# Hash attention and feed-forward on one core: another start of attention, and hash bits on column halves kept on the chip in place of column quarters placed by transfers

## The chip, the cores and the metric

The kernel runs on one core of one Trainium2 chip. The metric is the device time of one execution in microseconds (us); the time before is the median of three runs. The engines are TensorE (PE, matrix products; PEld is its weight load), VectorE (DVE), ScalarE (ACT), GpSimd (POOL) and SyncE (SP, which here only issues transfers). Each engine works through its own instructions in order and waits on semaphores for the others.

## The reference, cut to what matters

```python
batch, n_heads, seq, head_dim = (4, 8, 768, 64)      # q, k, v; proj is 64 x 6
q_bits = (np.einsum('bhsd,dk->bhsk', q, proj) > 0)   # 6 hash bits of each query
k_bits = (np.einsum('bhsd,dk->bhsk', k, proj) > 0)   # and of each key
q_bucket = np.sum(q_bits * 2 ** np.arange(6), axis=-1)
k_bucket = np.sum(k_bits * 2 ** np.arange(6), axis=-1)
mask = q_bucket[:, :, :, None] == k_bucket[:, :, None, :]
scores = np.where(mask, scale * np.matmul(q, k.transpose(0, 1, 3, 2)), -1e9)
attn = softmax(scores)                               # over the keys
x = np.matmul(attn, v)                               # then reshaped to 3072 x 512
# feed-forward: n_tokens, d_model, d_ff = (3072, 512, 2048)
h = x @ w_in
g = h * erf(softplus(h))
out = g @ w_out
```

## The kernel before

The heads are worked on in 16 pairs (a and b). q and k of a pair lie one head on partitions 0 to 63, the other on 64 to 127. A half is 384 of the 768 queries, HS = 384. A score block is 128 keys by 384 queries of both heads; a pair has 12 of them. Each block is four matrix products in one PSUM tile: two that put the mask there, made of bits, and two in fp32 with q and k. ACT takes the exp of it, and the product with v (`weigh`) sums over the keys. The score tiles and the bits share one ring of three PSUM tiles.

```python
QR = 32
QB = QR // 2
WARM = 7
...
nc.vector.memset(w_sum[:, 0, 0, 0:HS], 1.0)
warm = w_sum[:, 0, 0, 0:HS].bitcast(BF16)
proj_in = const.tile([P, 2 * NBIT], F32, name="proj_in")
nc.scalar.dma_start(out=proj_in, in_=proj2)
...
def fetch(i, load, quick=False):
    ...
    for half in range(2 if quick else 1):
        cols = slice(half * HS, half * HS + HS) if quick else slice(0, S)
        for n, what in enumerate("qk"):
            queue = nc.scalar if quick and what == "k" and half == 0 else nc.sync
            for ab in range(2):
                queue.dma_start(...)
    # then v, by nc.sync
```

The first pair takes its bits on column halves, one half of the sequence after the other: two products into the tile `bits` (q to partitions 0 to 63, k to 64 to 127), the sign by ACT, and three small DVE operations.

```python
def hash_bits(d, big, halves=(0, 1)):
    if halves[0] == 0:
        d["bits"] = big("bits")
    for half in halves:
        for n, what in enumerate("qk"):
            nc.tensor.matmul(out=d["bits"][n * D : n * D + D, half, 0:HS], lhsT=proj_sb,
                             rhs=d[what][:, half * HS : (half + 1) * HS], start=True, stop=True)

def take_bits(d, tile_of, halves=(0, 1)):
    cols = slice(halves[0] * HS, (halves[-1] + 1) * HS)
    sign_bits(d, tile_of, cols)            # ACT
    for ab in (1, 0):
        spread_bits(d, cols, ab)           # DVE, scaled by a weight
    double_bits(d, cols)                   # DVE copy

def score(n, c):
    ...
    st = d["st", n, c] = big("st")
    for part, src in enumerate(("b", "")):     # "b": mask in bf16, "": q and k in fp32
        for ab in range(2):
            rows = slice(ab * D, ab * D + D)
            nc.tensor.matmul(out=st[:, ab, 0:HS], lhsT=d["k" + src][rows, keys],
                             rhs=d["q" + src][rows, cols], start=(part == 0), stop=(part == 1))
...
pairs[0] = fetch(0, load, quick=True)
for n in range(WARM):
    nc.tensor.matmul(out=bank("warm"), lhsT=warm[:, 0:P], rhs=warm[:, P : P + 512], start=True, stop=True)
for half in range(2):
    hash_bits(pairs[0], big, (half,))
    take_bits(pairs[0], lambda what: both[0][:, "qk".index(what[0]), :], (half,))
```

All later pairs take them on column quarters: four products side by side, one sign, one DVE scaling, a store to memory, and two loads that place the bits where the mask product wants them.

```python
def bits_of(i):
    d["bits"] = big("bits")
    for n, what in enumerate("qk"):
        for half in range(2):
            row = (2 * n + half) * QR
            nc.tensor.matmul(out=d["bits"][row : row + QR, 0, 0:HS], lhsT=proj_q,
                             rhs=d[what][:, half * HS : (half + 1) * HS], start=True, stop=True)

def sign_of(i):      # ACT Sign, 128 x 384, into sg
def weigh_bits(i):   # DVE, sg[64:128] times weight_q
def leave_bits(i):   # POOL queue: sg to memory
def place_bits(i):   # POOL queue: two loads into both[i % 2]
def clean():         # POOL clears both[0] once
```

A list scheduler in the kernel fixes the order of all engines ahead of time from costs that are written in it; PE's own order is a fixed chain, which for half h holds the score blocks, in every other half the bits of the next pair, the divisor of the half before, and `weigh`.

```python
order = [("score", 0)]
for h in range(NH):
    order += [("score", n) for n in (2 * h + 1, 2 * h + 2) if n < NS]
    if h == 0:
        order.insert(3, ("bits", 1))
    if h % 2 and (h + 3) // 2 < NPAIR:
        order.append(("bits", (h + 3) // 2))
    if h >= 1:
        order.append(("divisor", h - 1))
    order += [("weigh", 2 * h), ("weigh", 2 * h + 1)]
```

Beside attention DVE and ACT split the float64 weights into fp32 (32 pieces). The feed-forward follows when attention ends.

Of the kernel before, what the change touches and what calls it, by code (L numbers as in the profile page):

```python
# [193 lines left out]
def kernel(  # L194
# [36 lines left out]
    QB = QR // 2  # L231
    WARM = 7
    proj_sb = const.tile([P, 2 * QR], F32, name="proj_sb")
    weight = const.tile([P, 2], F32, name="weight")
    proj_q = const.tile([P, QR], F32, name="proj_q")
    weight_q = const.tile([P, 1], F32, name="weight_q")
# [12 lines left out]
    warm = w_sum[:, 0, 0, 0:HS].bitcast(BF16)  # L249
    proj_in = const.tile([P, 2 * NBIT], F32, name="proj_in")  # L250
    nc.scalar.dma_start(out=proj_in, in_=proj2)
# [9 lines left out]
    steps = const.tile([P, 8], F32, name="steps")  # L261
    for c, (end, factor) in enumerate(
        (
            (NBIT, NBIT + 1.0),
            (NBIT + 1, -float(NBIT)),
            (QR, -1.0),
            (QR + NBIT, NBIT + 1.0),
            (QR + NBIT + 1, -float(NBIT)),
            (QB, -1.0),
            (QB + NBIT, NBIT + 1.0),  # L270
            (QB + NBIT + 1, -float(NBIT)),
        )
    ):
        nc.vector.tensor_scalar(
            out=steps[:, c : c + 1],
            in0=row,
            scalar1=float(end),
            scalar2=factor * BIG,
            op0=ALU.is_lt,
            op1=ALU.mult,  # L280
        )
    nc.vector.reduce_sum(out=weight[:, 0:1], in_=steps[:, 0:2], axis=AX.X)
    nc.vector.reduce_sum(out=weight[:, 1:2], in_=steps[:, 2:5], axis=AX.X)
    nc.vector.memset(proj_q, 0.0)
    for ab in range(2):
        rows = slice(ab * D, ab * D + D)
        nc.vector.tensor_copy(
            out=proj_q[rows, ab * QB : ab * QB + NBIT],
            in_=proj_in[rows, ab * NBIT : (ab + 1) * NBIT],
        )  # L290
    nc.vector.reduce_sum(out=weight_q, in_=steps[:, 5:8], axis=AX.X)
    nc.vector.tensor_tensor(out=weight_q, in0=weight_q, in1=weight[:, 0:1], op=ALU.add)
    nc.vector.tensor_copy(out=weight_q[D + QR : P, :], in_=weight_q[D : D + QR, :])
# [52 lines left out]
    def fetch(i, load, quick=False):  # L346
        d = dict(
            q=load.tile([P, S], F32, name="q", tag="q"),
            k=load.tile([P, S], F32, name="k", tag="k"),
            v=load.tile([P, NC, P], F32, name="v", tag="v"),  # L350
        )
        b, j = divmod(i, JP)
        for half in range(2 if quick else 1):
            cols = slice(half * HS, half * HS + HS) if quick else slice(0, S)
            for n, what in enumerate("qk"):
                queue = nc.scalar if quick and what == "k" and half == 0 else nc.sync
                for ab in range(2):
                    queue.dma_start(
                        out=d[what][ab * D : ab * D + D, cols],
                        in_=qkT[2 * i + ab, n * D : n * D + D, cols],  # L360
                    )
        for ab in range(2):
            nc.sync.dma_start(
                out=d["v"][:, :, ab * D : ab * D + D],
                in_=v[b, 2 * j + ab].rearrange("(c p) d -> p c d", p=P),
            )
        return d

    def hash_bits(d, big, halves=(0, 1)):
        if halves[0] == 0:  # L370
            d["bits"] = big("bits")
# [10 lines left out]
    def sign_bits(d, tile_of, cols):  # L382

        if cols.start == 0:
            for what in ("qb", "kb"):
                d[what] = tile_of(what)
# [23 lines left out]
    def take_bits(d, tile_of, halves=(0, 1)):  # L410
        cols = slice(halves[0] * HS, (halves[-1] + 1) * HS)
        sign_bits(d, tile_of, cols)
# [4 lines left out]
    def attention():  # L417
        NS = NPAIR * 4
        with (
            tc.tile_pool(name="load", bufs=3) as load,  # L420
            tc.tile_pool(name="bitp", bufs=1) as bitp,
            tc.tile_pool(name="ep", bufs=1) as ep,
            tc.tile_pool(name="xst", bufs=1) as xst,
# [8 lines left out]
            sg = bitp.tile([P, HS], BF16, name="sg")  # L432
            both = [bitp.tile([P, 2, S], BF16, name=f"both{n}") for n in range(2)]
            nc.gpsimd.memset(both[1], 0.0)
# [102 lines left out]
            def score(n, c):  # L537
# [5 lines left out]
                st = d["st", n, c] = big("st")  # L543
                for part, src in enumerate(("b", "")):
                    for ab in range(2):
# [7 lines left out]
                        )  # L553

# [33 lines left out]
            def sum_keys(h, k):  # L588
                i, half = divmod(h, 2)
                d = pairs[i]  # L590
                if k == 0:
                    if h >= NH - 2:
                        if half:
                            room = blocks[1][:, :, :].rearrange("p k t -> p (k t)")[:, 0:S]
                        else:
                            room = load.tile([P, S], F32, name="q", tag="q")
                        d["sum", half] = room.rearrange("p (n a c) -> p n a c", n=1, a=2)
# [34 lines left out]
            def home(i, what):  # L632

                if i < NPAIR - 1:
                    shape, bufs = {"x": (S, 3), "z": (HS, 1), "r": (S, 2)}[what]
                    return xst.tile([P, shape], F32, name=what, tag=what, bufs=bufs)
                rows = blocks[1][:, :, :].rearrange("p k t -> p (k t)")
                c = {"x": S, "z": 2 * S, "r": 0}[what]
                return rows[:, c : c + (HS if what == "z" else S)]
# [132 lines left out]
            for n in range(WARM):  # L772
                nc.tensor.matmul(  # L773
                    out=bank("warm"),
                    lhsT=warm[:, 0:P],
                    rhs=warm[:, P : P + 512],
# [3 lines left out]
            for half in range(2):  # L780
                hash_bits(pairs[0], big, (half,))
                take_bits(pairs[0], lambda what: both[0][:, "qk".index(what[0]), :], (half,))
# [14 lines left out]
            def bits_of(i):  # L797


                d = pairs[i]  # L800
                d["bits"] = big("bits")
                for n, what in enumerate("qk"):
                    for half in range(2):
                        row = (2 * n + half) * QR
                        nc.tensor.matmul(  # L805
                            out=d["bits"][row : row + QR, 0, 0:HS],
                            lhsT=proj_q,
                            rhs=d[what][:, half * HS : (half + 1) * HS],
                            start=True,
                            stop=True,  # L810
                        )

            def sign_of(i):
                nc.scalar.activation(
                    out=sg,
                    in_=pairs[i].pop("bits")[:, 0, 0:HS],
                    func=AF.Sign,
                    scale=2.0**100,
                    bias=sgn[:, 0:1],
                )  # L820

            def weigh_bits(i):

                nc.vector.tensor_scalar(
                    out=sg[D:P, :],
                    in0=sg[D:P, :],
                    scalar1=weight_q[D:P, 0:1],
                    scalar2=None,
                    op0=ALU.mult,
                )  # L830

            def leave_bits(i):
                bd = pairs[i]["bd"] = dram.tile([4, 2, QB, HS], BF16, name="bd", tag="bd")
                nc.gpsimd.dma_start(out=bd.rearrange("n a r c -> (n a r) c"), in_=sg)

            def place_bits(i):

                d = pairs[i]
                bd = d.pop("bd")
                for n, what in enumerate(("qb", "kb")):  # L840
                    d[what] = both[i % 2][:, n, :]
                for ab in range(2):
                    nc.gpsimd.dma_start(
                        out=both[i % 2][ab * D : ab * D + NBIT + 1, :, :].rearrange(
                            "r w (h c) -> r (w h) c", h=2
                        ),
                        in_=bd[:, ab, 0 : NBIT + 1, :].rearrange("n r c -> r n c"),
                    )

            def clean():  # L850

                nc.gpsimd.memset(both[0], 0.0)
# [3 lines left out]
            for h in range(NH):  # L856
                order += [("score", n) for n in (2 * h + 1, 2 * h + 2) if n < NS]
                if h == 0:
                    order.insert(3, ("bits", 1))
                if h % 2 and (h + 3) // 2 < NPAIR:  # L860
                    order.append(("bits", (h + 3) // 2))
# [4 lines left out]
            for what, n in order:  # L866
                if what == "score":
                    i = n // 4
                    after = (("place_bits", i),)
                    for c in range(GC):  # L870
                        free = (slots[-3],) if len(slots) >= 3 else ()
                        pe(score, (n, c), 0.82, after + free)
                        slots.append(("exponential", n, c))
                elif what == "bits":
                    pe(bits_of, (n,), 0.92, (("start_pair", n), slots[-3]))
# [27 lines left out]
            for h in range(NH):  # L903
                for k, (blocks_, _, _, where) in enumerate(sum_steps(h)):
                    after = tuple(("exponential", 2 * h + b // GC, b % GC) for b in blocks_)
                    after += (("sum_keys", h, k - 1), ("sum_keys", h - 1, last_sum(h - 1)))
                    if k == 0:
                        after += (("divisor", h - 2),)
                        if h == NH - 2:
                            after += (("measure", NPAIR - 3, 0, 1),)  # L910
                    op(sum_keys, (h, k), "DVE", 1.72 if where == 2 else 0.92, (1, 2 * h + 1, k), after)
            for h in range(NH - 1):
# [7 lines left out]
                    (("divisor", h), ("spread", i - 1)),  # L920
# [6 lines left out]
            for i in range(NPAIR):  # L927
                n = 4 * i
                if i:
# [10 lines left out]
                    op(sign_of, (i,), "ACT", 0.6, (0, n - 6, 9), (("bits_of", i), ("leave_bits", i - 1)))  # L940
                    op(weigh_bits, (i,), "DVE", 0.33, (0, n - 6, 1), (("sign_of", i),))
                    op(leave_bits, (i,), "POOL", 0.7, (0, n - 6, 2), (("weigh_bits", i),), late=2.6)
                    op(
                        place_bits,
                        (i,),
                        "POOL",
                        1.2,
                        (0, n - 6, 3),
                        (("leave_bits", i), ("score", n - 5, 2)) + (("clean",),) * (i == 2),
                        late=2.6,  # L950
# [11 lines left out]
                if i == NPAIR - 1:  # L962
# [11 lines left out]
                    (("ungather", i), ("normalise", i - 2)),  # L974
# [4 lines left out]
            op(clean, (), "POOL", 1.4, (0, 0), (("score", 3, 2),), late=0.3)  # L979
# [49 lines left out]
    def general():  # L1029

        with (
# [13 lines left out]
            for i in range(NPAIR):  # L1045
# [3 lines left out]
                take_bits(d, lambda what: bitp.tile([P, S], BF16, name=what, tag=what))  # L1049
# [704 lines left out]
```

## Time and profile before

| | |
|---|---|
| time, median of 3 runs | 919.47 us (918.86 to 923.69) |
| span of the profiled run | 917.7 us |
| first score block on PE | 9.58 us |
| first exp on ACT | 11.42 us |
| first product with v on PE | 18.90 us |
| last product with v ends on PE | about 324.6 us |

The page gives the busy time of each engine and its share of the span, the span in slices, and the chain of work that ended last, followed back from the last instruction. A timeline row has start, length, engine, line of the kernel, operation, what is written and read, how many were merged into the row, and in brackets how long the engine sat idle before it and what released it. The row "waits" has who waited for whom, the total in us, the times and the longest. Ends of matrix products are modelled, and merged rows overlap, so starts are safer to compare than lengths.

### The profile page before, as it was taken

The numbers are of one execution on the slowest core, as the hardware profiler recorded it, in microseconds if no ns is written. First come the engines' busy times: TensorE is split into PE (matmuls) and PEld (weight loads), VectorE is DVE, ScalarE is ACT, GpSimd is POOL, SyncE is SP. The second block draws the span as 40 slices with busy tenths as digits, with TensorE's granted clock in tenths as the row PEclk, the third lists the DMA queues.
The fourth block names the chain that finished last, engine by engine and source line by source line (L and its number), as shares of the span: only waits on it lengthen the run. The fifth ranks groups of instructions, "written<-read, shape, count | busy, mean of one in ns | idle before, by whom it ended". The sixth has DMA issues, their size and how long they took to land.

```text
span 917.7 us, 13114 instructions
## 1 busy us (share of the span) xinstructions
PE 904.2 (99%) x5003; PEld 657.1 (72%) x5003; DVE 820.2 (89%) x1020; ACT 768.2 (84%) x1002; POOL 46.1 (5%) x82
## 2 busy tenths in 40 slices
PE   8999999999999999999999999999999999999997
PEld 3444444444444478888888888888888888888885
DVE  4889999999999979899999799989899889988995
ACT  5788887788887839999998998899989997899892
POOL 1211111111111000000000000000000000000000
PEclk9999999999999999999999999999999999999999
DMA  8456567665574231102022112211221021111211
GB/s 205 114 155 163 144 178 194 184 161 164 155 190 138 59 122 64 46 1 104 12 70 80 36 46 69 81 35 46 70 81 35 35 75 40 36 35 46 69 35 49
DMA packets 63078, 83.05 MB, mean 90 GB/s; under 512 B 34286, under 2 KB 47454, under 8 KB 63008
## 3 DMA queue, kind: packets, MB, share of 16 engines
q1 hardware_dynamic: 56672, 64.08, 24.6%
q0 software_dynamic: 6032, 17.86, 6.3%
q8 instruction: 41, 0.67, 0.3%
q10 hardware_dynamic: 304, 0.20, 0.1%
q14 instruction: 29, 0.24, 0.1%
HBM read 64.71 MB, written 17.40 MB: 89 GB/s over the span
## 4 chain that ended last, share of the span: by engine, by line
PE 95%; DVE 2%; ACT 1%; DMA 1%; issue 0%; POOL 0%; DVEq 0%; POOLq 0%
PE M L1313 31%; PE X L1173 28%; PE st L547 16%; PE av L624 14%; PE M L1173 3%; PE z_ps L659 1%; PE bits L805 1%; ACT e_all L561 1%; PE warm L773 0%; DVE e L1227 0%; PE bits L374 0%; DMA bd<-sg 0%; DVE h L1255 0%; DMA both<-bd 0%; DVE S L1270 0%
## 5 line engine op out<-in xcount | busy, mean ns | idle before, releaser
L1240 DVE SCALAR_TENSOR_TENSOR e<-w,e 128x1024 f32<-128x1024 f32 x144 | 173.3, 1219 | 5.8 <-ACT w L1236 3.0
L561 ACT ACTIVATE e_all<-st 128x768 f32<-128x768 f32 x192 | 151.5, 813 | 14.2 <-PE st L547 12.8
L1236 ACT ACTIVATE w<-w,cq 128x1024 f32<-128x1024 f32 x144 | 160.6, 1143 | 1.9
L547 PE MATMUL st<-q,k 64*128 64x384 f32 x768 | 156.1, 485 | 0.0
L1313 PE MATMUL M<-w_out_sb,h 128*128 128x256 f32 x576 | 140.2, 379 | 0.4 <-DVE h L1255 0.4
L624 PE MATMUL av<-e_all,v 128*64 128x385 f32 (+1 forms) x768 | 131.2, 490 | 0.0
L1173 PE MATMUL X<-x,w_in_sb 128*128 128x256 f32 x512 | 121.1, 379 | 0.0
L1313 PEld LDWEIGHTS M<-w_out_sb,h 128*128 128x128 f32 x576 | 109.3, 190 | 15.9 <-DVE h L1255 1.1
L1173 PEld LDWEIGHTS X<-x,w_in_sb 128*128 128x128 f32 x512 | 97.0, 190 | 13.8 <-ACT h L1191 0.6
L624 PEld LDWEIGHTS av<-e_all,v 128*64 128x64 f32 x768 | 52.3, 136 | 67.5 <-issue 65.4
L547 PEld LDWEIGHTS st<-q,k 64*128 64x128 f32 x768 | 68.8, 189 | 35.1 <-issue 34.8
L1313 PE MATMUL M<-wt,S 128*128 128x256 f32 x384 | 93.4, 379 | 0.4 <-DVE S L1270 0.4
L1173 PE MATMUL X<-x_sum,w_sum 128*128 128x256 f32 x344 | 81.7, 380 | 1.8 <-ACT h L1191 1.8
L1313 PEld LDWEIGHTS M<-wt,S 128*128 128x128 f32 x384 | 72.9, 190 | 10.7 <-DVE S L1270 0.8
L1173 PEld LDWEIGHTS X<-x_sum,w_sum 128*128 128x128 f32 x344 | 65.0, 190 | 12.0 <-ACT h L1191 3.3
L1191 ACT COPY h<-X 128x512 f32<-128x512 f32 x85 | 49.1, 577 | 22.3 <-PE X L1173 21.4
L1217 DVE SCALAR_TENSOR_TENSOR w<-w,e 128x1024 f32<-128x1024 f32 x48 | 58.4, 1220 | 9.7 <-ACT w L1212 9.6
L547 PE MATMUL st<-both 64*128 64x384 bf16 x384 | 63.7, 326 | 1.6 <-DMA both<-bd 1.0
L1255 DVE TENSOR_TENSOR h<-h,e 128x1024 f32<-128x1024 f32 x48 | 57.9, 1220 | 5.8 <-ACT e L1251 5.6
L1231 ACT ACTIVATE w<-e 128x1024 f32<-128x1024 f32 x48 | 50.4, 1050 | 13.2 <-DVE e L1227 13.0
L1227 DVE TENSOR_TENSOR e<-e,w 128x1024 f32<-128x1024 f32 x48 | 57.4, 1218 | 2.7 <-ACT e L1223 2.6
L1195 DVE TENSOR_TENSOR h<-X,h 128x512 f32<-128x512 f32 x65 | 44.8, 689 | 16.4 <-PE X L1173 15.4
(132 smaller groups left out, 1373.8 us busy)
## 6 DMA issues: line engine op xcount, KB each, us to landing
wt<-wt SPq DMA_DIRECT2D x24, 768.0 KB, 4.2
raw<-in_w_out_dram POOLq DMA_DIRECT2D x16, 512.0 KB, 4.1
raw<-in_w_in_dram POOLq DMA_DIRECT2D x14, 512.0 KB, 4.9
v<-in_v_dram SPq DMA_DIRECT2D x32, 192.0 KB, 4.7
xs<-x SPq DMA_DIRECT2D x16, 384.0 KB, 3.2
q<-in_qkT_dram SPq DMA_DIRECT2D x30, 192.0 KB, 4.2
k<-in_qkT_dram SPq DMA_DIRECT2D x30, 192.0 KB, 4.5
r<-rd SPq DMA_DIRECT2D x30, 192.0 KB, 3.5
```

What stands on the lines that cost most here:

```text
L547: nc.tensor.matmul(out=st[:, ab, 0:HS], lhsT=d["k" + src][rows, keys], rhs=d["q" + src][rows, cols], start=(part == 0), stop=(part == 1),)
L561: nc.scalar.activation(out=e[:, :, 0:HS], in_=st[:, :, 0:HS], func=AF.Exp, scale=scale)
L624: nc.tensor.matmul(out=d["av"][rows, 0:w], lhsT=d["v"][:, g * GC + c, rows], rhs=e[:, ab, 0:w], start=(g == 0 and c == 0), stop=(g == 1 an ...
L1173: nc.tensor.matmul(out=d[where][:, u, :], lhsT=a[:, kc, f : f + P], rhs=b[:, kc, :], start=(first and u == 0 and kc == 0), stop=(last and ...
L1191: nc.scalar.copy(out=quarter(p, q), in_=st[p][where])
L1217: nc.vector.scalar_tensor_tensor(out=w, in0=w, scalar=-1.0, in1=st[p]["e", v], op0=ALU.add, op1=ALU.subtract)
L1227: nc.vector.tensor_tensor(out=s, in0=s, in1=st[p].pop(("w", v)), op=ALU.subtract)
L1231: nc.scalar.activation(out=z, in_=st[p]["s", v], func=AF.Square)
L1236: nc.scalar.activation(out=q, in_=z, func=AF.Square, bias=cq[:, j : j + 1])
L1240: nc.vector.scalar_tensor_tensor(out=s, in0=st[p].pop(("q", v, j)), scalar=ERF_Q[j][1], in1=s, op0=ALU.add, op1=ALU.mult,)
L1255: nc.vector.tensor_tensor(out=h, in0=h, in1=st[p].pop(("s", v)), op=ALU.mult)
L1313: nc.tensor.matmul(out=banks[name][:, sub, :], lhsT=a[:, u, sub * P : (sub + 1) * P], rhs=b[:, u, :], start=(c == 0 and k == 0), stop=(c = ...
```

## The change: what it does and what it is for

At the start: the warm-up products on constants become fp32 and are five of 256 columns, so that they follow each other with no gaps; the projection is loaded by POOL's queue; the loads of the second half of the first pair take k ahead of q; the first pair's bits go to two PSUM tiles, one for each half, so that the second half's products don't wait for the first half's sign; and the first two score blocks run their fp32 products first and take their masks last, so that PE has work while the bits are made.

For the later pairs it goes back to bits on column halves that stay on the chip: four products of which two run side by side, one sign of 128 x 768, two DVE scalings and one DVE copy. The store, the two loads, the quarter constants and the clears go away. Some buffers become fewer (x from three to two; z and r share two), and the order of a few operations in the scheduler changes with them.

```diff
-    QB = QR // 2
-    WARM = 7
+    WARM = 5
...
-    warm = w_sum[:, 0, 0, 0:HS].bitcast(BF16)
+    warm = w_sum[:, 0, 0, 0:HS]
...
-    nc.scalar.dma_start(out=proj_in, in_=proj2)
+    nc.gpsimd.dma_start(out=proj_in, in_=proj2)
... (steps for the quarters, proj_q and weight_q go away)
-        for half in range(2 if quick else 1):
-            cols = slice(half * HS, half * HS + HS) if quick else slice(0, S)
-            for n, what in enumerate("qk"):
+        parts = ((0, "q"), (0, "k"), (1, "k"), (1, "q")) if quick else ((None, "q"), (None, "k"))
+        for half, what in parts:
...
     def hash_bits(d, big, halves=(0, 1)):
-        if halves[0] == 0:
-            d["bits"] = big("bits")
+        d["bits"] = big("bits")
...
-            tc.tile_pool(name="bitp", bufs=1) as bitp,
+            tc.tile_pool(name="bitp", bufs=2) as bitp,
             tc.tile_pool(name="ep", bufs=1) as ep,
-            tc.tile_pool(name="xst", bufs=1) as xst,
+            tc.tile_pool(name="sums", bufs=2) as sums,
+            tc.tile_pool(name="xst", bufs=2) as xst,
...
-            def score(n, c):
+            def score(n, c, parts=((0, "b"), (1, ""))):
...
-                st = d["st", n, c] = big("st")
-                for part, src in enumerate(("b", "")):
+                if ("st", n, c) in d:
+                    parts = ((1, "b"),)
+                else:
+                    d["st", n, c] = big("st")
+                st = d["st", n, c]
+                for part, src in parts:
...
+            def plain(n, c):
+                score(n, c, ((0, ""),))
...
-                    shape, bufs = {"x": (S, 3), "z": (HS, 1), "r": (S, 2)}[what]
-                    return xst.tile([P, shape], F32, name=what, tag=what, bufs=bufs)
+                    return xst.tile([P, S], F32, name=what, tag="x" if what == "x" else "z")
...
-                    out=bank("warm"),
+                    out=bank("warm")[:, 0 : 2 * P],
                     lhsT=warm[:, 0:P],
-                    rhs=warm[:, P : P + 512],
+                    rhs=warm[:, P:HS],
...
             def bits_of(i):
-                ... four products with proj_q, each to 32 partitions
+                hash_bits(pairs[i], big)
             def sign_of(i):
-                ... Sign of 128 x 384 into sg
-            def weigh_bits(i): ...
-            def leave_bits(i): ...
-            def place_bits(i): ...
-            def clean(): ...
+                sign_bits(pairs[i], bitp, slice(0, S))
+            def weigh_bits(i, ab):
+                spread_bits(pairs[i], slice(0, S), ab)
+            def copy_bits(i):
+                double_bits(pairs[i], slice(0, S))
...
-                if h == 0:
-                    order.insert(3, ("bits", 1))
-                if h % 2 and (h + 3) // 2 < NPAIR:
-                    order.append(("bits", (h + 3) // 2))
+                if h % 2 == 0 and h // 2 + 1 < NPAIR:
+                    order.append(("bits", h // 2 + 1))
...
+                    if n == 0:
+                        for c in range(2):
+                            pe(plain, (n, c), 0.66)
...
-                    (("divisor", h), ("spread", i - 1)),
+                    (("divisor", h), ("send", i - 1) if i == NPAIR - 1 else ("widen", i - 1)),
```

## The prediction

> **What bounds the kernel now.** I read the page's busy row and chain of waits first, then the windows of 20 us over the attention part, the waits of TensorE (PE), the timeline of one pair of heads, and last the timeline of the first 20 us.
>
> ```profile
> PE 904.2 (99%) x5003; PEld 657.1 (72%) x5003; DVE 820.2 (89%) x1020; ACT 768.2 (84%) x1002; POOL 46.1 (5%) x82
> ...
> PE 95%; DVE 2%; ACT 1%; DMA 1%; issue 0%; POOL 0%; DVEq 0%; POOLq 0%
> ```
>
> PE is busy 99% of the span and is 95% of the chain that ended last. Work added to PE's in-order chain is therefore paid in full, and work on another engine is free until PE waits for it. By stretch (columns: stretch, length, busy of PE, PEld, DVE, ACT, POOL with counts, clock, DMA share, GB/s):
>
> ```profile
> 20.00:40.00 20.00, 19.02 (x142) 9.07 (x140) 16.77 (x23) 16.74 (x33) 5.88 (x9) 1.00 0.51 133
> 40.00:60.00 20.00, 20.00 (x148) 9.31 (x150) 18.38 (x28) 17.06 (x32) 3.40 (x6) 1.00 0.52 126
> ...
> 300.00:320.00 20.00, 20.00 (x146) 9.18 (x141) 18.99 (x28) 16.62 (x30) 0.56 (x1) 1.00 0.23 67
> ```
>
> From 40 us to the end of attention (325 us) PE has almost no gap; the only large one is 1 us between 20 and 40 us. Attention alternates halves with a hash product and halves without. The product with v (av) starts each half's last part, so the distance of its starts is a half's length. PE timeline (columns: start, length, instruction):
>
> ```profile
> 275.02 4.10 PE L624 MATMUL av<-e_all,v 128*64 128x385 f32 x24
> ...
> 284.01 0.52 PE L805 MATMUL bits<-q,proj_q 128*32 128x384 f32 x2
> 284.02 0.52 PE L805 MATMUL bits<-k,proj_q 128*32 128x384 f32 x2
> 284.35 0.49 PE L805 MATMUL bits<-q,proj_q 128*32 128x384 f32 x2
> 284.37 0.49 PE L805 MATMUL bits<-k,proj_q 128*32 128x384 f32 x2
> 284.68 0.51 PE L659 MATMUL z_ps<-x_sum,ones 128*32 128x192 f32 x8
> 285.11 4.09 PE L624 MATMUL av<-e_all,v 128*64 128x384 f32 x24
> ...
> 294.55 4.10 PE L624 MATMUL av<-e_all,v 128*64 128x385 f32 x24
> ```
>
> With the hash product a half lasts 285.11 - 275.02 = 10.09 us, without it 294.55 - 285.11 = 9.44 us. The product costs **0.65 us** of PE net. Its four matrix products (q and k, two halves of columns) are two instructions each, and all four run side by side: two rounds of 0.33 us.
>
> The start (PE timeline again):
>
> ```profile
> 1.40 4.45 PE L773 MATMUL warm<-w_sum 128*128 128x512 bf16 x7 [1.40 <-DVE w_sum L248]
> 5.78 0.90 PE L374 MATMUL bits<-q,proj_sb 128*64 128x384 f32 x1
> ...
> 8.03 0.90 PE L374 MATMUL bits<-q,proj_sb 128*64 128x384 f32 x1 [0.71 <-ACT both L387]
> ...
> 9.58 0.50 PE L547 MATMUL st<-both 64*128 64x384 bf16 x2
> 9.88 1.49 PE L547 MATMUL st<-q,k 64*128 64x384 f32 x4
> 11.16 0.53 PE L547 MATMUL st<-both 64*128 64x384 bf16 x2
> 11.48 1.05 PE L547 MATMUL st<-q,k 64*128 64x384 f32 x4
> 12.37 0.32 PE L547 MATMUL st<-both 64*128 64x384 bf16 x2
> ```
>
> Three things are to be seen. The warm-up leaves holes (0.64 us from one to the next for 512 columns). The second half's bits wait for the Sign of the first half, since both halves share one PSUM tile. And PE runs at half pace until about 11.4 us: the same four fp32 products last 1.49 us at 9.88 and 0.81 us from 12.54 on, so the first two score blocks take 2.8 us instead of 1.6.
>
> **What the Trainium skill says.** "TensorE: Matmul & The Clock Gate", Part 3 (packing small matmuls), says that products in different column groups run at the same time. The trace agrees: 10 to 20 ns lie between the starts of q and k quarters. Part 1 of that page says that the array runs at 1.2 GHz until a free-running window of about 3.4 us was busy, then at 2.4. The trace agrees in size: a bits round is 0.69 us at 5.78 us (to 6.47) and 0.33 us at 284. That a warm-up with holes doesn't count as busy fits (7 of them over 4.45 us left PE slow), but this trace alone doesn't prove it. "DMA: Bandwidth & Descriptors", Anatomy of one DMA, puts some 2 us of fixed cost on any transfer; here the bits' trip to memory takes 3.4 us (median) and the trip back 4.0.
>
> **The change, part by part.**
>
> (a) Later pairs (15 of them): hash bits on column halves again. q takes columns 0-63 and k 64-127, so two products run together and not four: two rounds for each half of the sequence, four rounds in all, 4 x 0.33 = 1.3 us instead of 0.65. Added on PE: 0.65 x 15 = **+9.7 us**, all on the path. ACT's Sign grows from 128x384 (0.59 us) to 128x768 (estimate 0.85, from the exp of that shape at 0.81): +0.27 x 15 = 4 us, where ACT has some 3.5 of 20 us free. DVE loses one 64x384 scaling (0.32) and gets two of 64x768 and a copy of 64x768: between 1.2 us (the costs that the kernel's own scheduler is given) and 1.8 us (twice the 0.32 and 0.25 of the short ones); about +0.9 to 1.5 a pair, 13 to 22 us in all. DVE's idle time from 20 to 320 us is about 20 us by the windows, and attention becomes some 8 us longer. It stays just inside.
>
> (b) Removed: the trip of the bits through memory (one store, two loads a pair) and two clears of the bits' tile on POOL. Only where PE waits for it does this pay:
>
> ```profile
> PE st L547 <- DMA both<-bd: 1.0, 2, 0.7
> ```
>
> That is pair 1, at 26 us. Score blocks start 0.81 us apart; after the one at 24.56 the next but one was due at 26.18 and started at 27.58, so the loss is about **1.4 us**. For later pairs the bits are ready long before. In the new kernel pair 1's bits have two products with v's block (4.0 us) and three score blocks (2.4 us) ahead of their first use, 6.5 us, against a chain of Sign 0.9 + DVE 1.2 to 1.8 plus queues: no wait. Gain -1.4.
>
> (c) The start. The warm-up becomes 5 fp32 products of 256 columns. A bits instruction of 384 columns is 0.65 us apart when slow, so one of 256 is 0.43, ten of them 4.3 us: the end stays near 5.7 us, but without holes, so the fast clock should come between 5 and 8 us and not at 11.4. First bits in two tiles: the second half follows at once (0.65 us less wait) if its loads are there; by the DMA rate (about 690 KB moved at 5.25 us of the 774 KB ahead) they land near 6 to 6.5. Two score blocks then start with their fp32 part and need no bits: 1.3 us of work under the Sign and DVE chain of half 0 (1.6 us in the trace, 7.38 to 8.95). By sum: bits 5.7 to 7.5, plain parts to 9.0, masks, first exp near 9.2 instead of 11.42. Then ACT sets the pace with nine exp of 0.81, so not all of this arrives: the first av product starts perhaps 1.3 to 2.5 us earlier. I take **-1.9 us**. The projection now loads by POOL's queue and the k of half 0 leaves ACT's queue 0.4 us earlier; both land before the warm-up ends.
>
> (d) Buffers: x has two and not three, z and r share two. The store of x for pair 3 is issued at 118.65 and lands 3.5 us later (median), 122.2; the copy that would now need this buffer ran at 122.93. So there is little slack, but ACT was idle 2.4 us before that copy, and PE has three score tiles in hand. I allow **+0.3 us** for this, for the later keep of the divisors and for the fuller DVE.
>
> Feed-forward from 325 us on isn't touched. Sum: 919.5 + 9.7 - 1.4 - 1.9 + 0.3 = **926.2 us**.
>
> **The rivals.** First: the memory trip was the real cost, and its removal plus the start outweighs the products; then 914 to 918. Against it stands that PE's waits for these transfers are 1.0 us in all and its windows are full. Second: DVE becomes the bound of attention. It has 93% in the windows from 20 to 320 us, and the added 13 to 22 us could make divisors or bits late; each pair would then lose another 0.5 us or more, and the time would go to 932 to 938. For it: the idle time left is small. Against it: some 116 us of its work (the seven operations that split the weights, 32 times 3.6 us) is weight conversion with low rank, which can slip to 325-340 us, where DVE has over 4 us free in 20; the sums are done some 7 us ahead (277.9 for the divisor at 284.7). Third: ACT waits for a buffer or a divisor copy in order, and PE runs out of score tiles: +0.5 us a pair, 930 to 934. Fourth: the fast clock doesn't come earlier, the start brings nothing or only the overlap: 927 to 928.
>
> **Range and chances.** The PE term is sure within 1 us, the start within 1.5, the queue effects only push upward by up to 4. So **926.2 us, 922.5 to 930.5**; 2% is 18 us, which only the DVE rival at its worst reaches: faster 0.01, same 0.96, slower 0.03.
>
> **What would show it.** Bits products of later pairs as four rounds, 1.3 us; av starts 10.7 us apart with bits and 9.4 without; no wait at 26 us; first exp near 9.2 and first av near 17.5 to 18; warm-up at one piece, PE fast by 8 us; DVE over 95% in attention with PE still 20.00 of 20. Wrong would be: PE windows under 19.8 in mid attention, waits of PE for weighed bits or for z_ps, or a bits group that costs well under 1.3 us.

## The result and the profile after

The changed kernel takes **932.53 us** (median, 931.83 to 933.51), the kernel before 920.59 us beside it: ratio **1.0127**, 95% interval 1.0095 to 1.0158. It is slower by 12 us; predicted were 926.2 us, 922.5 to 930.5. The direction was right; a loss of 6.7 us was foreseen, a little over half of it.

The busy row and the chain, on the page of the changed kernel:

```profile
PE 916.4 (98%) x5006; PEld 663.1 (71%) x5006; DVE 829.2 (89%) x1041; ACT 770.7 (83%) x1002; POOL 18.2 (2%) x36
...
PE 81%; DVE 11%; DMA 3%; ACT 2%; issue 2%; DVEq 0%; SPq 0%; ACTq 0%
```

PE got 12.2 us more work, and its share of the chain fell from 95% to 81%: DVE and transfers now stand in the chain, which is a sign of new waits. By stretch (same columns as in the prediction):

```profile
40.00:60.00 20.00, 20.00 (x146) 9.15 (x144) 19.04 (x29) 16.30 (x28) 2.06 (x3) 1.00 0.38 100
...
140.00:160.00 20.00, 19.62 (x142) 9.21 (x140) 16.16 (x26) 14.98 (x29) 0.65 (x2) 1.00 0.50 140
...
280.00:300.00 20.00, 19.25 (x138) 8.91 (x136) 17.94 (x25) 14.60 (x29) 1.05 (x2) 1.00 0.58 153
```

Most stretches are full, a few in mid attention are not; there DVE is not full either. A half with bits and one without, on PE's timeline:

```profile
48.68 4.09 PE L609 MATMUL av<-e_all,v 128*64 128x384 f32 x24
...
57.66 0.54 PE L357 MATMUL bits<-q,proj_sb 128*64 128x384 f32 x1
...
58.03 0.49 PE L357 MATMUL bits<-q,proj_sb 128*64 128x384 f32 x1
...
58.35 0.49 PE L357 MATMUL bits<-q,proj_sb 128*64 128x384 f32 x1
...
58.67 0.49 PE L357 MATMUL bits<-q,proj_sb 128*64 128x384 f32 x1
...
59.10 0.53 PE L642 MATMUL z_ps<-x,ones 128*32 128x192 f32 x8
59.56 4.10 PE L609 MATMUL av<-e_all,v 128*64 128x385 f32 x24
```

Four rounds, as foreseen; but the half takes 59.56 - 48.68 = 10.88 us, not 10.7, and the next one 9.44. The bits cost 1.44 us net where they cost 0.65. The start, on the timeline of all engines:

```profile
1.40 6.34 PE L756 MATMUL warm<-w_sum 128*128 128x256 f32 x10 [1.40 <-DVE w_sum L245]
...
2.67 0.50 PEld L756 LDWEIGHTS warm<-w_sum 128*128 128x128 f32 x2 [0.78 <-PE warm L756]
...
7.67 0.90 PE L357 MATMUL bits<-q,proj_sb 128*64 128x384 f32 x1
...
11.81 5.93 ACT L550 ACTIVATE e_all<-st 128x768 f32<-128x768 f32 x8 [1.06 <-PE st L532]
```

The warm-up has its holes after all: each weight load waits for the product before it, a product comes every 1.28 us and not every 0.85, and the bits start at 7.67 us, 1.9 us later than before. The first exp is at 11.81 (11.42 before).

From here on I use three marks of each trace: the start of the first av product, the start of the feed-forward on PE ("FFN"), and the distances of av starts between them. FFN starts at 337.27 us, 12.14 us later than before (325.13). The feed-forward itself has the same waits in both traces; it takes 592.6 us in the one and 593.8 in the other, within the 592.5 to 594.2 of all sixteen traces.

### The profile page after: what moved, and what is told of

It reads as the page before. It is cut to its first block, busy times and chain, and to the rows that moved or that the text cites. A ratio compares the mean times of both kernels' runs of the same rounds, so it can differ in the third digit from the quotient of the medians.

```text
span 931.1 us, 13001 instructions
## 1 busy us (share of the span) xinstructions
PE 916.4 (98%) x5006; PEld 663.1 (71%) x5006; DVE 829.2 (89%) x1041; ACT 770.7 (83%) x1002; POOL 18.2 (2%) x36
## 4 chain that ended last, share of the span: by engine, by line
PE 81%; DVE 11%; DMA 3%; ACT 2%; issue 2%; DVEq 0%; SPq 0%; ACTq 0%
PE M L1248 30%; PE X L1108 27%; PE st L532 9%; PE av L609 8%; PE M L1108 3%; DVE x_sum L597 2%; DVE x L597 2%; PE bits L357 1%; DMA zd<-z 1%; DMA xs<-x 1%; ACT e_all L550 1%; PE z_ps L642 1%; DVE top L488 1%; DVE top L474 1%; DVE x L728 1%
## 5 line engine op out<-in xcount | busy, mean ns | idle before, releaser
L550 ACT ACTIVATE e_all<-st 128x768 f32<-128x768 f32 x192 | 148.8, 819 | 10.5 <-PE st L532 9.2
L1248 PEld LDWEIGHTS M<-wt,S 128*128 128x128 f32 x384 | 72.9, 190 | 10.7 <-DVE S L1205 0.8
L532 PE MATMUL st<-qb,kb 64*128 64x384 bf16 x384 | 62.9, 324 | 1.5 <-ACT e_all L550 1.5
L666 ACT COPY x<-av 128x384 f32<-128x384 f32 x32 | 15.3, 478 | 56.4 <-DMA xs<-x 26.9
```

The source lines that it names most:

```text
L550: nc.scalar.activation(out=e[:, :, 0:HS], in_=st[:, :, 0:HS], func=AF.Exp, scale=scale)
L1248: nc.tensor.matmul(out=banks[name][:, sub, :], lhsT=a[:, u, sub * P : (sub + 1) * P], rhs=b[:, u, :], start=(c == 0 and k == 0), stop=(c = ...
```

## The account of the 12 us

All from the distances of av starts. Before, 14 halves with bits at 10.09, 16 without at 9.44 to 9.45, the short last one at 7.02 and 4.67 from the last av start to FFN make 304.1 us; the trace has 306.2, so 2.2 us of waits. After, with 10.88, they make 315.1; the trace has 318.3, so 3.2 us of waits. The first av is at 18.96 against 18.90 although pair 1's bits take 0.56 longer (17.62 to 18.96 here, 18.12 to 18.90 before; no divisor stands between these bits and av), so in these two traces the start gained 0.5.

| term | predicted | measured |
|---|---|---|
| bits on halves, 15 pairs | +9.7 | +11.6 (14 x 0.79, pair 1 0.56) |
| old waits gone (pair 1's placed bits and one more) | -1.4 | -2.2 (1.5 of it pair 1) |
| start | -1.9 | -0.5 |
| new waits | +0.3 | +3.2 |
| sum | +6.7 | +12.1 |

Three theories were to be told apart. For the bits: PE time paid in full, plus a cost of switching between column halves and quarters. For the new waits: either the **two x buffers** (ACT must wait for a store of x, and behind it the exp and PE), or the **fuller DVE**, which brings x late. For the start: the warm-up's length, the time at which the fast clock comes, or a gain that the wait of pair 1 eats.

## The experiments

| kernel | us | ratio to before (95%) | first av | FFN |
|---|---|---|---|---|
| e1 new, third x | 932.12 | 1.0130 (1.0101 to 1.0158) | 20.07 | 338.19 |
| e2 new, sums moved only | 931.11 | 1.0123 (1.0097 to 1.0150) | 20.04 | 340.79 |
| e3 new, buffers of before | 931.13 | 1.0133 (1.0106 to 1.0160) | 18.92 | 335.47 |
| e4 before + new start | 919.71 | 1.0008 (0.9995 to 1.0021) | 18.65 | 324.51 |
| e5 new, divisor first | 930.75 | 1.0122 (1.0095 to 1.0150) | 19.63 | 336.18 |
| e6 new, lighter DVE | 934.14 | 1.0151 (1.0128 to 1.0173) | 19.23 | 339.98 |
| e7 before, quarters twice | 928.29 | 1.0093 (1.0067 to 1.0118) | 19.30 | 332.89 |
| e8 new, bf16 warm-up | 929.49 | 1.0104 (1.0083 to 1.0125) | 16.77 | 337.24 |
| e9 e4 with bf16 warm-up | 922.20 | 1.0031 (1.0020 to 1.0043) | 17.34 | 327.84 |
| e10 e9, pair 1's bits earlier | 919.13 | 1.0009 (0.9995 to 1.0022) | 19.13 | 324.45 |
| e11 e4 with 3 fp32 warm-ups | 922.16 | 1.0032 (1.0020 to 1.0044) | 16.90 | 327.30 |
| e12 new, three mends | 928.94 | 1.0106 (1.0084 to 1.0128) | 17.45 | 333.08 |
| e13 e9, pair 1 on halves | **917.39** | **0.9974 (0.9964 to 0.9984)** | 16.78 | 321.74 |
| e14 before, pair 1 on halves | 918.55 | 0.9984 (0.9974 to 0.9994) | 17.53 | 321.47 |

Each ratio is to the kernel before as run beside that kernel (medians 919.16 to 921.01 us), so the ratios compare better than the times. The traced executions of e2 (935.27 us) and e8 (932.44 us) took 4 and 3 us longer than the slowest of their others (930.1 to 931.2 and 929.2 to 929.7), so their traces show more waiting than those kernels usually have.

### What the bits cost: e7 and e5

e7 issues the quarter products of the kernel before twice:

```diff
-                for n, what in enumerate("qk"):
+                for n, what in enumerate("qkqk"):
+                    n = n % 2
```

> The kernel before with the quarter products of each pair issued twice (the same values again), nothing else: PE's two rounds become four without column halves, Sign, DVE and transfers as before. If PE's work is paid in full: halves with bits 10.74 us instead of 10.09 (+0.65), 15 pairs make +9.8, 929 us. If there is slack for it: under 925. What remains to the 10.88 of the new kernel is what column halves cost beside the four rounds.

```profile
40.06 4.10 PE L624 MATMUL av<-e_all,v 128*64 128x385 f32 x24
...
49.04 0.52 PE L806 MATMUL bits<-q,proj_q 128*32 128x384 f32 x2
...
50.35 0.51 PE L659 MATMUL z_ps<-x_sum,ones 128*32 128x192 f32 x8
50.79 4.09 PE L624 MATMUL av<-e_all,v 128*64 128x384 f32 x24
```

The half takes 10.73 us; four rounds in quarters cost 1.29 us, 0.65 more than two, and the time goes up by 7.3 us (ratio 1.0093). In the halves PE's work is paid in full; that 7.3 is less than the 9.8 expected is mostly that the longer bits cover 1.7 us of the old waits (the first and fifth av distance are 11.32 and 10.74 here, 11.56 and 10.86 before). What is left to 10.88, some 0.14 us, belongs to the column halves themselves.

e5 exchanges two entries of PE's order in the new kernel:

```diff
+                if h >= 1:
+                    order.append(("divisor", h - 1))
                 if h % 2 == 0 and h // 2 + 1 < NPAIR:
                     order.append(("bits", h // 2 + 1))
-                if h >= 1:
-                    order.append(("divisor", h - 1))
```

> The new kernel with one exchange in PE's order: the divisor's products (column quarters) before the bits (column halves) and not after, so that the bits stand right ahead of the product with v, which uses column halves too. Switch theory (a change between quarters and halves costs PE some 0.1 us, which explains why the bits cost 1.43 us and not 1.3): the halves with bits take 10.78 us instead of 10.88, 1.4 to 1.5 us less over 15 pairs, last av near 331. Rival (the 0.13 us is the longer first round and the weight loads): 10.88 as before, same time. Both: within 2 us of 932, since other waits vary by that much from run to run; the distance of the av starts decides.

```profile
49.20 4.09 PE L609 MATMUL av<-e_all,v 128*64 128x384 f32 x24
...
58.18 0.53 PE L642 MATMUL z_ps<-x,ones 128*32 128x192 f32 x8
...
59.66 0.49 PE L357 MATMUL bits<-q,proj_sb 128*64 128x384 f32 x1
...
59.98 4.05 PE L609 MATMUL av<-e_all,v 128*64 128x385 f32 x24
```

From the last bits round to the next instruction are 0.32 us here and 0.43 in the new kernel, where the divisor (quarters) follows the bits (halves). The half is 10.78, as the switch theory said; the halves without bits went to 9.39, so a pair takes 20.17 us and not 20.33. That is what a pair takes in e7 too (10.73 + 9.44): in this order the column halves cost no more than four rounds in quarters. "TensorEngine Tiling (Array Packing)" in the Trainium skill, Tiling Modes, says that a change of the tiling mode drains the array; the 0.11 us at this change fits that. New waits for the weighed bits (0.7 and 0.8 us) took part of it back, and the medians, 930.75 and 932.53, are not separated by their intervals: the trace shows the switch, the time doesn't.

### Where the new waits come from: e1, e2, e3, e6

In the new kernel ACT's copy of the next x waits for the store of the x two pairs before (ACT's timeline, then PE's):

```profile
146.63 0.48 ACT L666 COPY x<-av 128x384 f32<-128x384 f32 x1 [4.38 <-DMA xs<-x]
147.00 1.52 ACT L550 ACTIVATE e_all<-st 128x768 f32<-128x768 f32 x2
```

```profile
147.87 0.34 PE L532 MATMUL st<-qb,kb 64*128 64x384 bf16 x2 [0.38 <-ACT e_all L550]
```

e1 gives x its third buffer (with the sums of the last two halves where the kernel before has them, to make room), e2 only moves the sums, e3 takes all buffers and their order from the kernel before:

```diff
-                    return xst.tile([P, S], F32, name=what, tag="x" if what == "x" else "z")
+                    return xst.tile([P, S], F32, name=what, tag="x" if what == "x" else "z",
+                                    bufs=3 if what == "x" else 2)     # e2: 2
```

> The new kernel with a third buffer for x (room for it comes from putting the sums of the last two halves where the kernel before has them). In the new kernel ACT waited 26.9 us in 7 waits for the store of x, and PE lost some 2.3 us in mid attention right behind the longest of them. Buffer theory: ACT has no wait for this store left, every half without bits lasts 9.44 to 9.5 us, the av product of the last half starts 2 to 2.5 us earlier than 332.60 (at 330.1 to 330.6), time about 930. DVE theory (the bound is the fuller DVE, and the buffer only shows it): the waits of PE come back elsewhere, as waits for bits, divisors or for e_all, and the time stays within 1 us of 932.5.

> The control to the third buffer: the same move of the last two sums, but x with two buffers as in the new kernel. Buffer theory: 932 to 933, the waits for the store of x as before in the new kernel (some 27 us on ACT, some 2.3 us on PE in mid attention). DVE theory: the same. If this alone brought 2 us, the third buffer would not be the cause.

> The new kernel with all buffers of the kernel before (x three, z and r by themselves) and its order of the copy of the divisors and of the loads of r. Buffer theory: as with the third x alone, 330, perhaps up to 1 us less if the later copy of the divisors cost something (the av product of the last half waited 0.9 us at 332.6). DVE theory: within 1 us of 932.5. In all cases the halves with bits stay at 10.88 us, so it can't come below 928.

Waits of e2, then of e1 (total, times, longest):

```profile
ACT x L670 <- DMA xs<-x: 36.7, 9, 5.2
```

```profile
ACT x L670 <- PE av L612: 49.0, 29, 5.9
...
PE av L612 <- DVE ev L676: 2.1, 1, 2.1
```

With the third buffer no wait for the store is left; with two it is 36.7 us (26.9 in the new kernel). So the third buffer ends these waits. That it shortens the time is not shown. From the first av to FFN e2 takes 320.7 us, e1 318.1, e3 316.6 (1.4 us of waits left), but e2's trace is of a long execution; against the new kernel's own 318.3 e1 wins nothing and e3 1.7 us. In e1 2.1 us came back at another place: the last av waits for a small DVE operation behind a weight piece. The ratios of e1 to e3, 1.0123 to 1.0133, lie about that of the new kernel, 1.0127; for e1 this is what its rival, the DVE theory, had expected.

e6 relieves DVE instead. It leaves out two of the six DVE operations of each weight piece (so the weights lack their low word):

```diff
-                nc.vector.tensor_scalar(out=unit, in0=top, scalar1=SIGN_EXP, ...)
...
-                nc.vector.scalar_tensor_tensor(out=rest, in0=low.bitcast(U32), ...)
-                nc.vector.tensor_tensor(out=pieces[n][0], in0=top.bitcast(F32), in1=rest, op=ALU.add)
+                nc.vector.tensor_tensor(out=pieces[n][0], in0=both, in1=both, op=ALU.max)
```

> The new kernel with DVE relieved: of each weight piece the low word is left out (two of six DVE operations, 0.43 and 0.69 us, 36 us in all; the weights then lack their last bits; order of all engines unchanged). Fullness theory (the new waits of PE, 3.3 us, come from a DVE that is late with the division of x, so that ACT waits for the store of x): ACT's waits for that store shrink from 27 to under 5 us, PE has no wait in mid attention nor at the last av, FFN starts 2.5 to 3.5 us earlier against the first av than the 318.3 of the new kernel, 929. Buffer theory alone (two x buffers are too few whatever DVE does): the waits stay near 27 us and the FFN start at 318.

```profile
ACT x L653 <- DMA xs<-x: 25.1, 6, 6.4
...
DVE x L715 <- DMA r<-rd: 7.0, 4, 2.3
```

The waits stay (25.1 us, longest 6.4), PE has four of them in mid attention (2.4, 0.4, 0.9 and 0.7 us), and the time doesn't fall. As the cause of these waits the fullness theory, which was my second rival, **falls**: with DVE relieved by 34 us (795.6 us busy against 829.2) two x buffers still make ACT wait. That the chain of five small transfers between the divisor and the store sets this time is what the second line suggests (DVE now waits for r); it was not tested by itself.

### The start: e4, e8, e9, e10, e11, e13, e14

e4 puts the new start on the kernel before. Its edit is the start part of the change's own diff, as shown with the change.

> The kernel before with the new start alone (fp32 warm-up, projection by POOL's queue, k ahead of q, bits in two tiles, the first two blocks with masks last); quarter bits, transfers and buffers stay. If the steps add up: the first av product at 18.96 less 0.78 (the longer bits of pair 1), 18.2 instead of 18.90, the wait at 26 us stays (0.7 to 1.5 us), and the time is some 0.7 us under the kernel before, 919 to 920. If the start is worth the 1.9 us that I had predicted, 918; if its gain is lost at the wait for placed bits, the same time as before.

First av 18.65 (18.90), FFN 324.51 (325.13), ratio 1.0008: the start alone is worth nothing that can be measured. The warm-up was suspect. e8 puts the old one back into the new kernel, e9 into e4, and e11 shortens e4's:

```diff
-    WARM = 5                                   # e11: 3, still fp32
+    WARM = 7
-    warm = w_sum[:, 0, 0, 0:HS]
+    warm = w_sum[:, 0, 0, 0:HS].bitcast(BF16)
...
-                    out=bank("warm")[:, 0 : 2 * P],
-                    rhs=warm[:, P:HS],
+                    out=bank("warm"),
+                    rhs=warm[:, P : P + 512],
```

> The new kernel with the old warm-up (7 bf16 products of 512 columns) and all else of the new start. In the new kernel the five fp32 products took 1.28 us each (a hole of 0.4 us for the weight load in each) and ended at 7.7 us, against 5.85 before. If the warm-up's length set the start: bits begin near 5.9, first exp near 10.2 to 10.8 instead of 11.81, first av 18 to 18.5 instead of 18.96. If the fp32 warm-up brings the fast clock earlier (9.4 us against 11.4): the old one leaves PE slow for longer, first exp at 11 to 11.5, first av within 0.5 us of 18.96.

> The kernel before with the new start, but its own warm-up (7 bf16 products); quarter bits and buffers stay. The new kernel with this warm-up had its first av at 16.77, 2.2 us ahead of the same kernel with the fp32 one. If the start gain is real and kept: first av near 16.0 to 16.2, FFN start near 322.5, 916.5 to 917.5, under the kernel before by some 2 to 2.5 us. Rival (the gain is lost again, for pair 1 waits for its placed bits at a fixed time set by the transfers): FFN start 324 to 325, the time of the kernel before.

> The kernel before with the new start and three fp32 warm-up products instead of five: they end near 5.2 us and not at 7.7. If only the length of the warm-up counts, this is as good as the bf16 one: bits from about 5.3 to 5.8, first av near 16 to 16.5. If the fast clock follows from how long PE was busy in all, it may come later, 1 us or more worse: first av 17 to 18.

In e8 the bits begin at 5.78 us and not at 7.67, and the first av is 2.2 us earlier, at 16.77 (17.45 in e12, which has the same start); in e9 and e11 it is 1.3 and 1.75 us earlier than in e4. So the five fp32 products had cost what the rest of the start brought. In e8's trace the gain is lost again, with FFN at 337.24 as in the new kernel: 4.6 us of waits for exp and for the last av (32.3 us of waits for the store of x on ACT) take it back. But this is the long execution; the other three of e8 lie 2.2 us and more below the lowest of the new kernel (931.83), so there the gain may arrive. The intervals of the two ratios overlap, and it stays open. On the kernel before the gain doesn't arrive: e9 and e11 are **slower** than it by 3 us, with no x buffer missing. The stretches of e9 show why (columns as before; the number after POOL's count is PE's clock):

```profile
24.00:26.00 2.00, 0.00 (x0) 0.00 (x0) 1.97 (x3) 1.40 (x3) 1.96 (x3) 1.00 0.29 60
26.00:28.00 2.00, 0.76 (x3) 0.39 (x5) 1.97 (x3) 0.00 (x0) 1.07 (x2) 0.56 1.01 252
28.00:30.00 2.00, 2.00 (x9) 1.41 (x9) 0.70 (x1) 0.47 (x1) 0.00 (x0) 0.50 0.99 318
30.00:32.00 2.00, 2.00 (x10) 1.07 (x6) 0.00 (x0) 1.15 (x2) 0.00 (x0) 0.50 0.12 47
```

```profile
26.85 0.48 PE L550 MATMUL st<-both 64*128 64x384 bf16 x1 [2.88 <-DMA both<-bd]
```

PE reached pair 1's blocks earlier, but the placed bits came at 26.85 (26.27 before). Their store had left 1.4 us earlier (18.99 against 20.36), but POOL waited 4.50 us for it to land and not 3.14, so the loads behind it left when they had before (the kernel before, then e9):

```profile
24.05 1.14 POOL L843 DMA_DIRECT2D both<-bd  x2 [3.14 <-DMA bd<-sg]
```

```profile
24.04 1.14 POOL L850 DMA_DIRECT2D both<-bd  x2 [4.50 <-DMA bd<-sg]
```

In PE's gap of 2.9 us its clock fell to half until about 33 us. The first av interval grew from 10.09 to 16.59 us: 3.3 us of waiting and as much again at half clock.

e10 moves pair 1's bits one group of three blocks earlier:

```diff
-                    order.insert(3, ("bits", 1))
+                    order.insert(2, ("bits", 1))
```

> As the one before, and pair 1's quarter bits go three score blocks (2.4 us) earlier in PE's order, so that their trip through memory ends before PE needs them. If the 1.4 us wait of pair 1 is all that this start leaves: first interval of av starts 10.09 or less in place of 11.2 to 11.6, FFN start 321 to 321.5, 915 to 916, the fastest of all. If pair 1's loads are not there yet so early, PE waits at the bits instead and nothing is won.

A miss: PE then waited 1.31 us for a score tile that the sign of the bits still held, the first av came at 19.13, and the time is that of the kernel before. e13 and e14 give pair 1 alone its bits on column halves on the chip, with the new start of e9 and with the old start:

```diff
+                if i == 1:
+                    return hash_bits(d, big)          # then sign, two scalings, copy into both[1]
...
-            nc.gpsimd.memset(both[1], 0.0)            # now cleared after pair 1's last block
```

> The kernel before with the new start, its bf16 warm-up, and pair 1 alone taking its bits on column halves on the chip (no trip through memory; the bits' tile is cleared after pair 1 and not ahead of it). Pairs 2 to 15 stay on quarters. If the start's gain is real and was eaten by the wait for placed bits (2.9 + 0.4 us, then half clock to 33 us): no wait of PE near 27 us, full clock there, first av near 17 to 18, FFN start 321.5 to 322.5, 915.5 to 917, faster than the kernel before by 2 to 4 us. If the start brings nothing: 918 to 920.

> The control: the same pair 1 on column halves, with the old start. The wait of 1.4 us near 26 us goes, and pair 1's products take 0.8 us more: FFN start 324 to 325 (325.13 before), 918 to 919.5, so 0 to 1 us under the kernel before. The difference to the run above is what the new start is worth when nothing eats it.

Stretches of e13:

```profile
20.00:40.00 20.00, 20.00 (x150) 9.39 (x146) 18.67 (x26) 16.40 (x31) 4.26 (x6) 1.00 0.53 130
```

No wait of PE is left between 20 and 40 us, and both are faster than the kernel before: e13 by 0.26% (0.16 to 0.36%), e14 by 0.16% (0.06 to 0.26%). e13 beats both kernels. The first av is at 16.78 with the new start and 17.53 with the old: in traces where the fast clock came at about the same time (just before 7 us in both) the start is worth 0.75 us. Of this 0.75 nothing is left at FFN, which is 0.27 us later in e13 than in e14: e13 waits 1.0 us for an exp in its fifth av distance (11.11). The medians are 1.2 us apart, but the intervals of the ratios overlap, so the start's share of the time is not settled. In e14 FFN at 321.47 is some 3 us ahead of what was expected. Most of that is not the edit's doing: the fast clock came earlier than in the trace of the kernel before, whose start is the same, and the second of the old waits did not occur.

### The mends together: e12

e12 is the new kernel with e3's buffers, e5's order and e8's warm-up; the edits are those shown.

> The new kernel with three mends together: buffers of the kernel before, divisor ahead of the bits, bf16 warm-up. Column halves stay. If my account of the 12 us is whole: about 2.2 (start) + 2.4 (0.16 a pair) + 1.8 to 3 (waits) less than the new kernel's FFN start of 337.27, so 330 to 331, and 925 to 926; what is left above the best form on column quarters is 15 times the two rounds, 0.65 us, some 9.8 us. If something else than the bits holds the new kernel back, it stays at 928 or more.

FFN at 333.08, 4.2 us earlier than in the new kernel, of which 1.5 are the start and the rest orders and waits; 928.94 us, a miss of 3 us against my 925 to 926. Two waits for the weighed bits (1.1 us) and some short ones remain, 2.7 us together by the av distances, though the x buffers are those of before: so a part of the new waits has another cause, which stays open. The ratio, 1.0106, is that of e8 with the warm-up alone (1.0104); buffers and order show no gain in the time. Against e13, which has the same start, FFN is 11.3 us later; 14 pairs at 20.17 instead of 19.53 us make 9.0 of these. The column halves for pairs 2 to 15 stay the bulk of the loss.

## Why the prediction was wrong, point by point

**The bound** was read rightly: PE's work is paid in full in the halves (e7: four rounds for two, 0.65 us a pair).

**Step (a)** had the right mechanism and a term too small: 1.3 us a pair, where 1.43 were measured. "4 x 0.33" counted the rounds and not the change from halves to quarters after them. The 0.65 us of before came without that cost, for bits and divisor there both use quarters. Over 15 pairs this is 1.9 us (11.6 for 9.7).

**Step (b)** held: the wait of pair 1 went, 1.5 us by the av distances against 1.4. A second old wait, 0.77 us in the fifth av distance (10.86), had been passed over; it went too.

**Step (c)** failed in its premise, "without holes". The products were spaced 1.28 us, the bits began at 7.67 and not at 5.7, and 0.5 us were gained instead of 1.9. I had taken the distance of instructions with loads hidden, from products of another kind, for products whose loads were not hidden. The other premise, that holes in the warm-up keep PE at half pace until 11.4 us, failed too: e14 has the same warm-up with the same holes and was at full pace before 8 us.

**Step (d)** failed most: 0.3 allowed, 3.2 found in the trace. I had the margin of the x buffer in hand (122.2 against 122.93 for one pair) and waved it off with ACT's idle time and the three score tiles. ACT's order is fixed: the copy that waits 4.4 us holds up the exp behind it, and three tiles are 2.4 us of PE. A margin of 0.7 us behind a chain of five transfers was no margin. How much of the 3.2 us the buffers caused is open: with all of them back, 1.4 us of waits stayed in e3 and 2.7 in e12, and the time of e3 did not fall.

**The rivals.** The third, ACT waiting in order for a buffer, was right in kind, if not in every pair. That its 930 to 934 holds the measured time is luck: it meant 0.5 us of waiting a pair, where 3.2 us were found in all, and bits and start made up the rest. The DVE rival gave a fitting figure too, and e6 refutes it as the cause of the waits for the store; single waits of PE for DVE are there (0.9 us in the new kernel, 2.1 in e1, 1.1 in e12). The bits' DVE work came out at the low end of the estimate, 1.19 us a pair (two scalings of 0.42, a copy of 0.35). The "seven operations" of a weight piece are six. The first, a win by the removed transfers, is out for the whole change, but holds for pair 1 (e14). The sum of the three misses, 1.9 + 1.4 + 2.9 less the 0.8 that the old waits gave beyond my figure, is 5.4 us, which closes the gap in the FFN start (12.1 to 6.7).

## What to carry to other kernels

Put a transfer between two products only where nothing needs its result soon: on quarters with transfers the later pairs are 0.64 us better (e13 against e12), and for the first one that PE runs into, the same trip is a loss. When a change takes a buffer away, take the margin from the worst pair and ask what stands behind the waiting instruction in its engine's order, rather than how idle that engine is. And an earlier start is worth only what the next fixed event lets through; look for that event before adding up gains.

## What was not expected of the hardware

- A gap of 2.9 us on PE cost about twice itself: the clock column has 0.50 from 26 or 27 to some 33 us (e9, e11), and the av distance grew by 6.5 us. The Trainium skill, "TensorE: Matmul & The Clock Gate", Part 1, says that one idle window of about 3.4 us brings the slow clock back; here 2.9 us were enough.
- Two executions with the very same first instructions got the fast clock at different times: the bits rounds of the second half are 0.70 us apart in the kernel before (at 8.03 us) and 0.37 in e14 (at 7.86). With this the first av came at 17.53 in e14 and at 18.90 before, though e14's bits of pair 1 take 0.56 longer: that leaves 1.9 us to the clock's timing. First av starts of e1, e2 and the new kernel (20.07, 20.04, 18.96), whose starts are alike, differ by 1.1 us in the same way. So one trace can't value a start to better than 1 to 2 us. The clock column is no help there: it has 1.00 for the first 20 us of the kernel before.
- A change from column halves to quarters on PE took about 0.1 us (0.43 us from the last bits round to the divisor in the new kernel, 0.32 to av in e5).
- fp32 warm-up products with 128 columns of weights had a hole of 0.43 us each (1.28 us less 0.85 for two instructions, an estimate from the bits' 0.64 us for 384 columns at this pace), while the bits' products on 64 columns followed each other every 0.64 to 0.69 us with no such hole. Why the one load was hidden and the other not wasn't tried.
